# mLSTM and gated feed-forward on one core: the second group's queries are transposed by VectorE from squares, and its scores move behind block 9

## The chip, the cores and the metric

The kernel runs on one core of a Trainium2 chip. The core has a matrix engine (TensorE, "PE" in the profile, whose weight loads are listed as "PEld"), a vector engine (VectorE, "DVE"), a scalar engine (ScalarE, "ACT"), GpSimd ("POOL") and a queue engine, SyncE ("SP"), which here only issues DMA transfers. The metric is the device time of one execution, in microseconds (us). Before the change it is 505.11 us, the median of three runs (504.91 to 505.61).

## The reference

An mLSTM cell goes over 768 time steps for 4 x 8 heads of width 40. Its output, joined over the heads into 3072 tokens of width 320, goes through a gated feed-forward block of width 1536.

```python
for t in range(S):
    m_new = np.maximum(f_gate[:, :, t] + m, i_gate[:, :, t])
    f_stab = np.exp(f_gate[:, :, t] + m - m_new)
    i_stab = np.exp(i_gate[:, :, t] - m_new)
    m = m_new
    C = f_stab[:, :, None, None] * C + i_stab[:, :, None, None] * np.einsum('bhd,bhe->bhde', vt, kt)
    n = f_stab[:, :, None] * n + i_stab[:, :, None] * kt
    h_tilde = np.einsum('bhde,bhe->bhd', C, qt)
    nq = np.einsum('bhd,bhd->bh', n, qt)[:, :, None]
    y[:, :, t] = o * h_tilde / np.maximum(np.abs(nq), 1.0)      # o: sigmoid of o_gate
...
x = y.transpose(0, 2, 1, 3).reshape(B * S, H * D)
g = x @ w_gate
return (g * (1.0 / (1.0 + np.exp(-g))) * (x @ w_val)) @ w_out
```

The cell's inputs are 32-bit floats, the three feed-forward weights 64-bit floats.

## The kernel before

**Stages.** Time is cut into six groups of 128 steps, 0 to 5. A group's tokens (4 batches x 128 steps = 512) go through the cell and then through the feed-forward block. The kernel writes out the order of every engine's work by hand: the feed-forward products of one group are the frame, and the cell's steps for the next group are put between them. The change is in the first frame, group 0's hidden products, into which group 1's cell is put.

**The frame.** `hidden(0, m)` is block m of twelve: ten matrix products (five chunks of x, gate and value half each) of 64 x 128 weights by 512 tokens into two PSUM banks (tile `gv_ps`, line 808), then Silu on ACT (line 813, into `tmp`) and the product with the value half on DVE (line 814, into `h_sb`). There are four such banks, so block m needs the banks that line 814 of block m - 2 has read. `first` is a list of steps issued between a block's matrix products and its Silu; `slots[m]` are steps issued after block m. `project_all` then makes group 0's output product (line 825), with more of the cell of groups 1 and 2 between its twelve parts (`after`).

**Weights.** The 64-bit weights are loaded in eleven pieces (`piece_load`): the gate part on SP's queue, the value part on POOL's. A piece of the later gate and value weights holds two blocks; piece 7 holds blocks 10 and 11, pieces 8 to 10 the output weights. A block is then turned into 32-bit floats in three steps: `scale` (two ACT instructions, lines 249 and 251, which read the piece and so wait for its load), `join` (two on DVE, 258 and 259) and `rounded` (one, line 266, on POOL or on DVE). `convert` is all three. Two raw buffers are shared by the pieces: piece 9 can be loaded when piece 7 has been scaled, piece 10 when piece 8 has.

**Group 1's cell in the frame.** k and q are loaded in their natural layout (128 steps on the partitions, heads and features along the row; line 139, rows of 160 bytes, two DMAs each). `turn_one` transposes them on TensorE, 16 transposes for each half P of the heads (line 378, tile `tp_kq`), and ACT copies the four banks to `kT` and `qT` (line 156). The weights of the attention come in `w_sb`, which is loaded by broadcast from `M_dram` (line 552, issued by SP after a small table has landed there); DVE caps it (`weights_cap`, line 570), subtracts (`weights_sub`, 559) and ACT takes the exponential (577). `do_scores` is 64 small matrix products of kT and qT (line 411, into four banks `sp`), `do_weigh` multiplies them into `w_sb` on DVE (line 418). `weigh_values` (POOL, line 422) weights v; `do_add` makes the state's products (line 437), `do_state` adds them (DVE, 461), `do_decayed` decays the state (POOL, 454); `do_intra` (478) and `do_inter` (468) make the outputs, `do_gather` joins them.

**Squares.** For groups 2 to 5, q is loaded in another form: `load_squares` issues, for each of the two heads of a pair, four DMAs with rows of 128 bytes and four with rows of 32 bytes (line 395), so that every 32 x 32 piece lies where VectorE can transpose it in place of TensorE; `turn_squares` is two VectorE transposes of 128 x 1024 (line 401). `q_sq` is the same memory as `q_sb`.

**The queues.** SP issues its DMAs in order. There are eight completion semaphores, taken in turn, so a DMA's issue waits for the landing of the one eight places before it. The order around the change is: k (2 DMAs), w_sb (2), q (2), the gate part of piece 7, v (2), pieces 8 and 9, o (2), group 2's q squares (8), piece 10, squares (8), group 2's w_sb (2).

## Time and profile before

| what | value |
|---|---|
| median of 3 runs | 505.11 us (504.91 to 505.61) |
| the profiled execution | 504.85 us, of which 503.1 us are its span |
| TensorE busy | 498.6 us, 99% of the span |
| VectorE, GpSimd, ScalarE busy | 333.2, 261.1, 209.2 us |
| granted TensorE clock | 1.00 in every stretch asked for from 24 to 108 us |
| group 0's hidden products, line 808 | first at 25.8 us, last at 86.1 us; 53.8 us busy |
| q transposes of group 1 on TensorE | 65.57 to 66.92 us |
| VectorE transposes, line 401 | 16, about 1.22 us each, first at 108.6 us |

The profile is one execution taken by the hardware profiler. Each row of a timeline gives the start and the duration, the engine, the line of the kernel, the operation with its tiles (`out<-in`), the shape and the number of instructions merged into the row; in brackets stands how long the engine was idle before and what ended that wait. An instruction's 32-bit product counts twice ("x20" for ten). The weight loads (PEld) run ahead of their products, and a small gap of 0.23 us between them is their normal step. In the slices of the page each digit is a busy share in tenths of 12.6 us. "SPq" rows are DMAs being issued; their time includes waiting for room in the queue.

### The profile page before, as it was taken

How to read it: one execution, taken by the hardware profiler on the slowest of the kernel's cores; microseconds unless marked ns; L12 is line 12 of the kernel's file. 1: busy time of each engine (PE TensorE's matmuls, PEld its weight loads, DVE VectorE, ACT ScalarE, POOL GpSimd, SP SyncE). 2: the span in 40 equal slices, each digit the busy share in tenths (PEclk: the TensorE clock that was granted, in tenths of full speed). 3: DMA queues.
4: the chain of work that ended last, by engine and by line, in shares of the span. 5: the costliest groups of instructions: out<-in, count | busy, mean ns of one | idle time of the engine just before them, and what ended most of it. 6: DMA issues, size and time to landing. Idle time of an engine off the chain costs nothing.

```text
span 503.1 us, 14945 instructions
## 1 busy us (share of the span) xinstructions
PE 498.6 (99%) x6361; PEld 424.4 (84%) x6361; DVE 333.2 (66%) x542; ACT 209.2 (42%) x406; POOL 261.1 (52%) x292
## 2 busy tenths in 40 slices
PE   9999999999999999999999999999999999999997
PEld 4856555767889899888899888899888899988897
DVE  5889869889998587578376677467468464233421
ACT  4776784476262266323247312339311330223210
POOL 3753525458876925465723357643267650176710
PEclk9999999999999999999999999999999999999999
DMA  9999998797607982404991502991101100000001
GB/s 145 194 231 244 160 210 215 169 167 115 88 3 120 157 85 52 44 3 68 165 115 45 67 3 47 161 128 27 42 3 25 32 1 27 27 1 1 1 14 39
DMA packets 184938, 43.29 MB, mean 86 GB/s; under 512 B 173128, under 2 KB 180312, under 8 KB 184360
## 3 DMA queue, kind: packets, MB, share of 16 engines
q1 hardware_dynamic: 183396, 38.00, 48.0%
q0 software_dynamic: 1344, 4.28, 3.6%
q8 instruction: 50, 0.82, 0.7%
q14 instruction: 16, 0.13, 0.1%
q10 hardware_dynamic: 132, 0.07, 0.0%
HBM read 35.68 MB, written 4.01 MB: 79 GB/s over the span
## 4 chain that ended last, share of the span: by engine, by line
PE 97%; DVE 1%; ACT 1%; issue 0%; DVEq 0%
PE gv_x L978 26%; PE o_ps L879 22%; PE gv_y L978 21%; PE gv_ps L808 10%; PE o_ps L825 5%; PE inter L468 2%; PE sp L411 2%; PE intra L478 2%; PE o_ps L884 1%; PE add L437 1%; PE tp_kq L378 1%; PE sp L641 1%; PE tp_x L543 1%; PE wps L609 1%; PE burn L587 0%; PE wps L613 0%
## 5 line engine op out<-in xcount | busy, mean ns | idle before, releaser
L978 PE MATMUL gv_x<-xT,wgv_sb 64*128 64x256 f32 x720 | 89.1, 377 | 0.0
L978 PEld LDWEIGHTS gv_x<-xT,wgv_sb 64*128 64x128 f32 x720 | 69.3, 187 | 8.1 <-issue 0.2
L879 PE MATMUL o_ps<-wo_sb,h_sb 128*128 128x160 f32 x456 | 63.9, 300 | 0.0
L879 PEld LDWEIGHTS o_ps<-wo_sb,h_sb 128*128 128x128 f32 x456 | 62.3, 190 | 1.7 <-issue 1.7
L1026 ACT ACTIVATE h_sb<-gv_x 128x256 f32<-128x256 f32 x30 | 11.5, 384 | 116.3 <-PE gv_x L978 116.3
L808 PE MATMUL gv_ps<-xT,wgv_sb 64*128 64x512 f32 x240 | 53.8, 596 | 0.0
L808 PEld LDWEIGHTS gv_ps<-xT,wgv_sb 64*128 64x128 f32 x240 | 26.7, 187 | 22.6 <-issue 14.9
L978 PE MATMUL gv_y<-xT,wgv_sb 64*128 64x256 f32 x360 | 43.9, 376 | 0.0
L978 PE MATMUL gv_y<-q_sb,wgv_sb 64*128 64x256 f32 x360 | 43.9, 376 | 0.0
L422 POOL TENSOR_TENSOR vw_sb<-v_sb,w_sb 128x656 f32<-128x656 f32 x10 | 14.6, 1464 | 51.0 <-ACT w_sb L574 38.1
L978 PEld LDWEIGHTS gv_y<-xT,wgv_sb 64*128 64x128 f32 x360 | 34.9, 187 | 4.0
L978 PEld LDWEIGHTS gv_y<-q_sb,wgv_sb 64*128 64x128 f32 x360 | 34.9, 187 | 4.0
L574 ACT ACTIVATE w_sb<-w_sb,g_T 128x64 f32<-128x64 f32 x128 | 31.0, 334 | 0.0
L978 PE MATMUL gv_x<-q_sb,sw 64*128 64x256 f32 x240 | 30.9, 376 | 0.0
L879 PE MATMUL o_ps<-wT,S 128*128 128x160 f32 x216 | 30.2, 299 | 0.0
L879 PEld LDWEIGHTS o_ps<-wT,S 128*128 128x128 f32 x216 | 29.6, 190 | 0.0
L1019 POOL TENSOR_TENSOR tmp<-tmp 128x512 f32<-128x512 f32 x15 | 20.0, 1334 | 16.8 <-DVE tmp L1018 16.8
L999 POOL TENSOR_TENSOR h_sb<-x_sb 128x512 f32<-128x512 f32 x12 | 15.7, 1306 | 24.6 <-ACT x_sb L998 24.6
L999 POOL TENSOR_TENSOR h_sb<-tmp 128x512 f32<-128x512 f32 x13 | 16.5, 1269 | 21.5 <-ACT tmp L998 21.5
L846 POOL TENSOR_TENSOR S<-h_sb 128x256 f32<-128x256 f32 x30 | 22.6, 755 | 9.2 <-DVE h_sb L999 7.3
L1018 DVE TENSOR_TENSOR x_sb<-x_sb,gv_y 128x1024 f32<-128x1024 f32 x15 | 18.1, 1205 | 13.9 <-PE gv_y L978 11.6
L825 PE MATMUL o_ps<-wo_sb,h_sb 128*128 128x320 f32 x96 | 27.1, 438 | 0.0
(238 smaller groups left out, 1004.7 us busy)
## 6 DMA issues: line engine op xcount, KB each, us to landing
w_sb<-M_dram SPq DMA_DIRECT2D x8, 512.0 KB, 6.6
raw<-in_moe_w_out_dram SPq DMA_DIRECT2D x3, 1280.0 KB, 7.1
v_sb<-in_v_dram SPq DMA_DIRECT2D x11, 320.0 KB, 9.4
o_sb<-in_o_gate_dram SPq DMA_DIRECT2D x11, 320.0 KB, 5.0
k_sb<-in_k_dram SPq DMA_DIRECT2D x9, 320.0 KB, 7.3
x_sq<-k_sb SPq DMA_DIRECT2D x64, 40.0 KB, 2.8
q_sb<-in_q_dram SPq DMA_DIRECT2D x32, 64.0 KB, 3.7
out_dram<-tmp SPq DMA_DIRECT2D x24, 80.0 KB, 1.7
```

The lines of the kernel that those rows point to most:

```text
L411: nc.tensor.matmul(sp[two][keys(n, P, i), a, :], lhsT=kT[feats(two), P * UA + a, half(i)], rhs=qT[feats(two), P * UA + a, half(i)], start= ...
L422: eng.tensor_tensor(vw_sb[:, heads(P)], v_sb[:, heads(P)], w_sb[:, heads(P), last].to_broadcast([128, UH, D1]), op=ALU.mult)
L574: nc.scalar.activation(w_sb[:, h], w_sb[:, h], AF.Exp, bias=g_T[:, n, h:h + 1], scale=-1.0)
L808: nc.tensor.matmul(ps[i], lhsT=wgv_sb[half(i), m, kc, :], rhs=x[half(i), kc, :], start=(kc == 0), stop=(kc == NKC - 1))
L825: nc.tensor.matmul(ps[u], lhsT=hid(g, m)[:, ts(u, L)], rhs=wo_sb[:, m, :], start=(m == 0), stop=(m == NFC - 1))
L846: eng.tensor_tensor(S1[:, k], lo[:, second_half], hi[:, second_half], op=ALU.add)
L879: nc.tensor.matmul(node[x][:, i], lhsT=lhs(k)[:, ts(i, L)], rhs=rhs(k), start=start and k == 0 and i == 0, stop=stop and k == KH - 1, skip ...
L978: nc.tensor.matmul(ps[:, i, cols], lhsT=lhs(c)[half(i)], rhs=rhs(c)[half(i)], start=start and c == 0, stop=stop and c == n - 1, skip_group ...
L999: (nc.vector if k == KH - 1 else nc.gpsimd).tensor_tensor(h_sb[:, 2 * k + 1], uw[:, 0], uw[:, 1], op=ALU.mult)
L1018: nc.vector.tensor_tensor(uw, uw, y, op=ALU.add)
L1019: nc.gpsimd.tensor_tensor(uw[:, :, second_half], uw[:, :, second_half], uw[:, :, first_half], op=ALU.add)
L1026: nc.scalar.activation(h[:, first_half], x[:, 0, first_half], AF.Silu)
```

## The change

Group 1's q is loaded as squares: eight DMAs behind block 2's steps, behind the k loads and ahead of w_sb, and eight behind block 3's, in place of two; the transposes on TensorE in the middle of block 8 (with the parameter `amid` that put them there) and their four ACT copies are gone, and two VectorE transposes stand behind block 7, after `weights_exp`. POOL no longer clears `q_sb` behind block 8 (the rows beyond the 40 features are read by no product). `do_scores` and `do_weigh` for group 1 move from behind block 8 to behind block 9. The conversion of block 10, which was issued whole ahead of block 8's Silu, has only its `scale` and `join` there; its `rounded` comes behind block 8's product of line 814, still on DVE.

```diff
-    def hidden(g, m, first=(), amid=()):
+    def hidden(g, m, first=()):
...
-            if kc == 3:
-                for f in amid:
-                    f()
...
-    on_vector = (9, 10)
-    ahead = {0: [], 1: [3], 2: [4], 3: [5], 4: [6], 5: [7], 6: [8], 7: [9], 8: [10], 9: [], 10: [], 11: []}
+    on_vector = (9,)
+    ahead = {0: [], 1: [3], 2: [4], 3: [5], 4: [6], 5: [7], 6: [8], 7: [9], 8: [], 9: [], 10: [], 11: []}
...
-        2: [run(late_maxima), run(M_store, G), run(load_all, k_sb, k, 1)],
-        3: [run(late_decay), run(weights_load, 1), run(load_all, q_sb, q, 1)],
+        2: [run(late_maxima), run(M_store, G), run(load_all, k_sb, k, 1), run(load_squares, q_sq, q, 1, (0,))],
+        3: [run(late_decay), run(weights_load, 1), run(load_squares, q_sq, q, 1, (1,))],
...
-        7: [run(weights_sub, 1, 0), run(weights_sub, 1, 1), run(weights_exp, 0), run(weights_exp, 1), run(weigh_values, G, 0),
-            run(weigh_values, G, 1)],
-        8: [run(nc.gpsimd.memset, q_sb, 0.0), run(do_scores, 1), run(piece_load, 9), run(load_all, o_sb, o_gate, 1),
-            run(do_weigh, 0), run(do_weigh, 1)],
-        9: [run(join, 11), run(rounded, 11, V), run(do_decayed, 2)],
+        7: [run(weights_sub, 1, 0), run(weights_sub, 1, 1), run(weights_exp, 0), run(weights_exp, 1),
+            run(turn_squares, q_sq, qT), run(weigh_values, G, 0), run(weigh_values, G, 1)],
+        8: [run(rounded, 10, V), run(piece_load, 9), run(load_all, o_sb, o_gate, 1)],
+        9: [run(do_scores, 1), run(do_weigh, 0), run(do_weigh, 1), run(join, 11), run(rounded, 11, V), run(do_decayed, 2)],
...
-    amid = {8: [run(turn_one, P, q_sb, qT, (A, A)) for P in range(2)]}
...
-        first += {9: [run(scale, 11)], 10: [run(scale, 12), run(join, 12)], 11: [run(convert, 13)]}.get(m, [])
-        hidden(0, m, first, amid.get(m, ()))
+        first += {8: [run(scale, 10), run(join, 10)], 9: [run(scale, 11)], 10: [run(scale, 12), run(join, 12)], 11: [run(convert, 13)]}.get(m, [])
+        hidden(0, m, first)
```

## The prediction

> **What bounds the kernel now.** First the page: span, busy time, the slices, the chain that ended last.

> ```profile
> span 503.1 us, 14945 instructions
> ...
> PE 498.6 (99%) x6361; PEld 424.4 (84%) x6361; DVE 333.2 (66%) x542; ACT 209.2 (42%) x406; POOL 261.1 (52%) x292
> ...
> DMA  9999998797607982404991502991101100000001
> ...
> PE 97%; DVE 1%; ACT 1%; issue 0%; DVEq 0%
> ```

> TensorE holds 97% of the chain, so a microsecond taken from it is a microsecond of the whole, as long as nothing else is late there. But a slice is 12.6 us: in the first eight or nine the DMA engines are nearly full too. So I read the timeline around the change (slices 5 to 9).

> ```profile
> 65.57 0.15 PEld L378 LDWEIGHTS tp_kq<-x_sq,q_sb 64*128 64x128 f32 x2 [0.23 <-issue]
> ...
> 66.92 0.31 PEld L808 LDWEIGHTS gv_ps<-xT,wgv_sb 64*128 64x128 f32 x4
> ...
> 68.20 2.03 ACT L156 COPY qT<-tp_kq 128x512 f32<-128x512 f32 x4
> 68.85 0.19 PEld L411 LDWEIGHTS sp<-qT,kT 40*64 40x64 f32 x2 [0.76 <-ACT qT L156]
> ...
> 70.74 0.79 ACT L249 ACTIVATE top<-raw 128x640 f32<-128x640 f32 x1 [0.51 <-DMA raw<-in_moe_w_gate_dram]
> 71.36 0.30 PEld L808 LDWEIGHTS gv_ps<-xT,wgv_sb 64*128 64x128 f32 x4
> ...
> 71.56 0.49 DVE L258 TENSOR_SCALAR wgv_sb<-top 128x640 uint32<-128x640 uint32 x1 [4.35 <-ACT top L249]
> ...
> 72.23 1.28 ACT L813 ACT_TABLE_LOAD   x1
> ...
> 73.05 1.71 DVE L266 CUSTOM_DVE_ANT_0 wgv_sb<-wgv_sb,low 128x1280 uint16<-128x1280 uint16 x1
> ...
> 73.53 0.60 ACT L813 ACTIVATE tmp<-gv_ps 128x512 f32<-128x512 f32 x1
> ...
> 75.33 0.25 PEld L808 LDWEIGHTS gv_ps<-xT,wgv_sb 64*128 64x128 f32 x2 [0.23 <-issue]
> ```

> Block 8 is cut by the transposes at 65.57 and resumes at 66.92; scores start at 68.85, block 9 at 71.36, block 10 at 75.33. Block 10's weights wait for a DMA (70.74) and are finished by DVE at 73.05 + 1.71 = 74.76, only 0.57 us before TensorE needs them. Next, SP's queue and the later place where TensorE meets a DMA again:

> ```profile
> 51.04 1.13 SPq L552 DMA_DIRECT2D w_sb<-M_dram  x2
> 52.22 5.56 SPq L139 DMA_DIRECT2D q_sb<-in_q_dram  x2
> 57.96 1.98 SPq L222 DMA_DIRECT2D raw<-in_moe_w_gate_dram  x1
> 59.99 9.73 SPq L139 DMA_DIRECT2D v_sb<-in_v_dram  x2
> ```

> ```profile
> 105.10 1.23 DVE L570 TENSOR_TENSOR w_sb<-w_sb,cap 128x1024 f32<-128x1024 f32 x1 [1.85 <-DMA w_sb<-M_dram]
> ...
> 107.73 2.40 POOL L266 TENSOR_TENSOR wo_sb<-wo_sb,low 128x640 int32<-128x640 int32 x1 [2.86 <-DVE wo_sb L259]
> ...
> 110.18 8.37 PEld L825 LDWEIGHTS o_ps<-wo_sb,h_sb 128*128 128x128 f32 x32 [0.41 <-POOL wo_sb L266]
> ```

> DVE waits 1.85 us for group 2's w_sb, the output weights' conversion stands behind that wait, and TensorE waits for it at 110.18.

> **The change, part by part.**

> *TensorE loses 32 transposes.* Pairs of weight loads step by 0.43 us. Without the cut, block 8's last four pairs take 65.57 to 67.29, block 9's ten to 71.59. The switch to small matmuls costs 0.52 (the last pair before the state products starts at 79.20, they at 80.15). 64 scores take 2.01, as the 64 state products do (80.15 to 82.16) and the third group's scores (130.24 to 132.26); here they took 2.51, since they waited for the qT copies. So block 10 could start at 72.11 + 2.01 = 74.12. The first two pairs after a switch take 0.54, not 0.86 (71.36, 71.90), so it would end at 74.12 + 4.30 - 0.32 = 78.10, against 75.33 + 4.30 = 79.63: a gain of 1.53 us, the most this change has on TensorE.

> *DVE gains two transposes,* 2 x 1.22 (L401 qT, x8, mean 1222 ns) = 2.44 us, behind weights_sub, which ends at 67.20. DVE stood idle from there to 71.56 (the 4.35 above), so they cost nothing while q is there by then. Scores need qT at 72.11; 67.20 + 2.44 = 69.64. *ACT loses* the 2.03 us of qT copies, but it waited for the gate weights anyway (0.51): nothing. *POOL loses* a 1.80 us memset; nothing on the path waits for POOL there: nothing.

> *Block 10's rounding moves behind block 8's product.* ACT's scaling of block 10 starts at T, now 70.74. It holds ACT until the table load at T + 1.49; the Silu of block 8 ends at 74.13 = T + 3.39; the product L814 (0.69) then stands ahead of the rounding L266, which was done beside the Silu before. L266 takes 0.83 alone (63.27) and 1.71 beside POOL's value weighting (72.35 for 3.57). Ready: T + 4.08 + 0.83 to 1.71 = T + 4.9 to T + 5.8; POOL covers about its first half, I take T + 5.5. With T unchanged that is 76.2, where TensorE could start at 74.12: it waits 2.1 us, more than the 1.53 gained. This is the step that decides; to keep the whole gain, T must be 68.6 or earlier, and the exponentials that ACT does first end at 68.29.

> *SP: two q DMAs become sixteen.* Eight go ahead of w_sb, eight between w_sb and the gate weights. Each DMA waits for the landing of the one eight before it. The eighth waits for the second k load (issued 30.68, landed after 21.4, 52.1), w_sb #1 for the first square (about 53). So w_sb is issued at about 53.5 instead of 51.04 and lands some 2.5 us later, near 60.3; DVE's cap, now at 59.52, starts 0.8 late. Behind it stand block 9's rounding (now done at 64.10, needed at 67.29: 3.2 us of cover) and the exponentials, which then end at 69.1. The last two squares wait for w_sb's landing, so the gate load is issued at about 61 instead of 57.96. That is not yet a loss: from 61.6 to 64.5 the DMA engines carried the val weights alone (q0 at 95%) and the gate packets came after, 65 to 68. T moves by what the DMA engines have to do before. Old q: 3560 packets in 4.0 us (57.3 to 61.3, share 155%), so 4.6 us for 4096. New: 4096 of 128 bytes and 4096 of 32. The same loads of group 2: 2105 packets, nearly all of 128 bytes, in 1.8 us (93.8 to 95.6, share 95%); 2131 small ones in 2.6 us at 62% share, 1.6 us of engine time, and 1850 in 3.2 us at 32%, 1.0 us. So 3.0 us a half if SP runs ahead, 6.0 in all, 1.4 more than now, less the hole between k and w_sb (51 to 53, share 45%: 1.1 us), which the first half fills: +0.3. If the packets come no faster than in the sparse rows, 2 x (1.8 + 2.6) = 8.8 us: 4.2 - 1.1 = +3.1. If the gate packets run beside the val packets, T falls, but not below the exponentials' end: 69.1, -1.6. I take +0.5, near the engine-time row, since in this window there is a backlog ahead and SP can push early: T = 71.2.

> [...] If the count alone set the time, 8192 packets at the old 890 per us would be 9.2 us, and T would be 3.5 us later; the 128-byte row (1170 per us) does not yet show that.

> *Sum on TensorE.* Ready at 71.2 + 5.5 = 76.7, 2.6 us after 74.12; less 1.53 gained: +1.05 at the end of block 10. Behind it the state products, block 11's weights and so on follow TensorE or have a microsecond of room. At 110.18 TensorE waited 0.41 for POOL; its loads there step by 0.27 with 0.19 busy, so about 0.3 is a true stall, which takes up 0.3: +0.75. The same place works the other way: its chain starts from w_sb's landing (105.0), reached by SP through a full DMA queue. Had TensorE kept its 1.53, it would wait there, unless group 2's w_sb came earlier too. In the profiled execution 504.85 + 0.75 = 505.6; the median shown is 0.26 above it: **505.9**.

> **Rivals.**

> *The gain is kept (faster).* The gate packets share the DMA engines with the val packets instead of following them, and the whole queue up to group 2's w_sb moves up by as much. For: from 40 to 44 us, when both queues had weights, they moved 307 GB/s, against 186 from 61.6 to 64.5. Against: it is the sum of bytes that group 2's w_sb waits for, and that does not shrink. With T = 69.1 and 5.0 behind it, block 10 starts at 74.1 and keeps the 1.53; with group 2's w_sb 1.3 earlier, the end is 505.1 - 1.3 = 503.8. It becomes a gain of 0.2% when both come 1.0 us earlier.

> *The DMA queue becomes the bound (slower).* T moves by the +3.1 above. Then block 10 starts at 79.3: 5.2 - 1.53 - 0.3 = +3.4, 508.5. For: group 2's second eight took SP 8.78 us (88.95), and 5.88 the first; with 7 us for each half, w_sb and gate come late by that. Against: there they stood behind 1.3 MB of output weights. From T + 0.75 on this is slower by over 0.2%.

> *DVE is blocked by a late q.* If the sixteenth square lands after 71.5, DVE's transposes hold back block 10's conversion. That square is issued near 61 and such loads landed within 2.1 to 4.4 us (median); 4 us more behind the val packets still leave 2 us. In the same case as the last.

> **How the numbers follow.** 0.2% is 1.0 us, about what a measurement of this kernel can tell from no change. Given back, 0.55: centre +0.75, with -0.2 to +2 from rounding alone or contended and T at +0.3 to +1.5; 0.32 of it within 1.0 us, 0.23 above. Kept, 0.17: 0.13 below -1.0, 0.04 within. Queue bound or q late, 0.28, all above. Together 0.13, 0.36, 0.51. The likeliest gives 505.9; its own range is 504.9 to 507.1. The range 504.0 to 508.2 leaves out half of the kept case and some of the bound one.

> **What would show it.** The scores' wait on ACT is gone and they take 2.0 us; DVE L401 appears twice ahead of block 10's L258. Right: a stall of 2 to 3 us on the matmuls' loads after the scores, ended by DVE's rounding, and the scaling of block 10 (ACT L249) waiting for the gate weights at 70.5 to 72. Wrong, to the fast side: no stall there, L249 before 69.5, and group 2's cap on DVE a microsecond earlier than 105.1. Wrong, to the slow side: w_sb landing after 62, or DVE waiting for q_sb ahead of L401.

## The result, and the profile after it

The changed kernel takes 509.76 us (median of six runs, 508.13 to 510.84) against 505.49 us for the kernel before beside it: ratio 1.0079, 95% interval 1.0054 to 1.0104. It is slower by 4.3 us. (The ratios here and below are worked out over the runs of both kernels and differ a little from the quotient of the two medians.) I had forecast 505.9 (504.0 to 508.2), so the sign was right and the size was not; the range did not hold it. The profiled execution took 508.92 us. Lines of the changed kernel are three lower than before (808 is 805, 813 is 810, 814 is 811, 825 is 822).

The page first: span, busy time, granted clock by slice, and the chain that ended last.

```profile
span 507.2 us, 14895 instructions
...
PE 499.1 (98%) x6329; PEld 425.2 (84%) x6329; DVE 334.4 (66%) x544; ACT 207.1 (41%) x402; POOL 258.7 (51%) x291
...
PEclk9999998999999999999999999999999999999999
...
PE 95%; DMA 2%; DVE 1%; ACT 1%; issue 0%; ACTq 0%; DVEq 0%
```

TensorE has 32 transposes less and is still busy 0.5 us longer, a DMA now holds 2% of the chain, and one slice has a granted clock below full speed (the 8 in the seventh, 76 to 89 us). The slice is right behind the changed place. The timeline there:

```profile
61.45 2.36 DVE L570 TENSOR_TENSOR w_sb<-w_sb,cap 128x1024 f32<-128x1024 f32 x2 [1.59 <-DMA w_sb<-M_dram]
...
68.82 2.36 DVE L401 STREAM_TRANSPOSE qT<-q_sb 128x1024 f32<-128x1024 f32 x2
...
72.05 0.78 ACT L249 ACTIVATE top<-raw 128x640 f32<-128x640 f32 x1 [2.05 <-DMA raw<-in_moe_w_gate_dram]
72.36 1.96 PEld L411 LDWEIGHTS sp<-qT,kT 40*64 40x64 f32 x128 [0.76 <-issue]
...
75.48 0.69 DVE L811 TENSOR_TENSOR h_sb<-tmp,gv_ps 128x512 f32<-128x512 f32 x1 [1.27 <-ACT tmp L810]
76.08 1.58 DVE L266 CUSTOM_DVE_ANT_0 wgv_sb<-wgv_sb,low 128x1280 uint16<-128x1280 uint16 x1
...
77.78 0.33 PEld L805 LDWEIGHTS gv_ps<-xT,wgv_sb 64*128 64x128 f32 x4 [3.46 <-ACT tmp L810]
77.81 6.26 PE L805 MATMUL gv_ps<-xT,wgv_sb 64*128 64x512 f32 x20 [3.35 <-DVE wgv_sb L266]
...
79.96 0.40 PEld L805 LDWEIGHTS gv_ps<-xT,wgv_sb 64*128 64x128 f32 x2 [0.45 <-issue]
80.81 0.40 PEld L805 LDWEIGHTS gv_ps<-xT,wgv_sb 64*128 64x128 f32 x2 [0.45 <-issue]
...
84.00 1.96 PEld L437 LDWEIGHTS add<-vw_sb,k_sb 64*64 64x64 f32 x128 [0.76 <-DVE wo_sb L258]
```

The scores run without a wait, from 72.36 to 74.32. Then TensorE stands for 3.4 us, until VectorE's rounding (L266) of block 10 ends at 77.66, and that chain starts at 72.05 with a wait for the gate weights. This is the stall that I had forecast, longer. The second thing I had not forecast: the pairs of weight loads of block 10 step by 0.85 us (79.96, 80.81) instead of 0.43, and the block needs 6.2 us from its start to the state products at 84.00 (4.8 before, from 75.33 to 80.15). The kernel before, at the end of block 10:

```profile
78.77 0.19 PEld L808 LDWEIGHTS gv_ps<-xT,wgv_sb 64*128 64x128 f32 x2 [0.24 <-issue]
79.20 0.19 PEld L808 LDWEIGHTS gv_ps<-xT,wgv_sb 64*128 64x128 f32 x2 [0.24 <-issue]
80.15 1.96 PEld L437 LDWEIGHTS add<-vw_sb,k_sb 64*64 64x64 f32 x128 [0.76 <-DVE wgv_sb L259]
```

```profile
71.55:74.96 3.41, 2.91 (x134) 2.01 (x130) 1.32 (x2) 2.88 (x4) 1.11 (x1) 1.00 1.44 174
74.96:78.37 3.41, 0.56 (x4) 0.39 (x6) 2.89 (x4) 2.31 (x4) 3.11 (x4) 1.00 1.07 365
78.37:81.78 3.41, 3.41 (x12) 1.60 (x10) 3.38 (x6) 0.00 (x0) 0.58 (x1) 0.50 0.94 337
81.78:85.20 3.42, 3.42 (x95) 2.04 (x92) 2.77 (x5) 2.64 (x4) 0.00 (x0) 1.00 1.12 220
```

In the stretch that holds the stall TensorE is busy for 0.56 us of 3.41; through the whole next one it gets half its clock. Half of 3.41 us is 1.7 us of work not done.

SP's queue, and the place at 105 to 110 us where TensorE met a DMA before:

```profile
54.19 1.13 SPq L552 DMA_DIRECT2D w_sb<-M_dram  x2
55.36 8.35 SPq L395 DMA_DIRECT2D q_sb<-in_q_dram  x8
63.88 2.25 SPq L222 DMA_DIRECT2D raw<-in_moe_w_gate_dram  x1
66.18 4.96 SPq L139 DMA_DIRECT2D v_sb<-in_v_dram  x2
```

```profile
107.01 1.21 DVE L570 TENSOR_TENSOR w_sb<-w_sb,cap 128x1024 f32<-128x1024 f32 x1
...
109.55 12.41 PEld L822 LDWEIGHTS o_ps<-wo_sb,h_sb 128*128 128x128 f32 x47
```

The second eight squares hold SP for 8.35 us; the gate load is issued at 63.9 (57.96 before). At 109.55 TensorE no longer waits for POOL, and the cap waits for no load: TensorE is late enough itself.

The 4.1 us of the span, by stages: block 0 starts 0.3 us later (26.2, 25.9 before), a place ahead of everything that the change touches; from there to the state products of group 1 it takes 3.55 us more (84.00 - 80.15 - 0.3); 0.2 of it is gone by the state products of group 2 (122.67 against 118.99); the rest of the span is 0.4 us longer. And the 3.55 add up: -1.53 (the gain as forecast) + 3.4 (stall) + 1.7 (half clock) = 3.57.

### The profile page after: what moved, and what is told of

It reads as the page before. It is cut to its first block, busy times and chain, and to the rows that moved or that the text cites. A ratio compares the mean times of both kernels' runs of the same rounds, so it can differ in the third digit from the quotient of the medians.

```text
span 507.2 us, 14895 instructions
## 1 busy us (share of the span) xinstructions
PE 499.1 (98%) x6329; PEld 425.2 (84%) x6329; DVE 334.4 (66%) x544; ACT 207.1 (41%) x402; POOL 258.7 (51%) x291
## 4 chain that ended last, share of the span: by engine, by line
PE 95%; DMA 2%; DVE 1%; ACT 1%; issue 0%; ACTq 0%; DVEq 0%
PE gv_x L975 26%; PE o_ps L876 21%; PE gv_y L975 21%; PE gv_ps L805 9%; PE o_ps L822 5%; PE inter L468 2%; PE intra L478 2%; PE sp L411 2%; DMA raw<-in_moe_w_gate_dram 2%; PE o_ps L881 1%; PE add L437 1%; DMA x_sq<-in_i_gate_dram 1%; PE tp_kq L378 1%; PE sp L641 1%; PE tp_x L543 1%; PE wps L613 1%
## 5 line engine op out<-in xcount | busy, mean ns | idle before, releaser
L876 PE MATMUL o_ps<-wo_sb,h_sb 128*128 128x160 f32 x456 | 63.9, 300 | 0.0
L805 PE MATMUL gv_ps<-xT,wgv_sb 64*128 64x512 f32 x240 | 55.2, 610 | 3.4 <-DVE wgv_sb L266 3.4
L805 PEld LDWEIGHTS gv_ps<-xT,wgv_sb 64*128 64x128 f32 x240 | 28.7, 192 | 26.3 <-issue 14.2
L1015 DVE TENSOR_TENSOR tmp<-tmp,gv_y 128x1024 f32<-128x1024 f32 x15 | 18.1, 1205 | 13.7 <-PE gv_y L975 12.0
```

Of the source, the lines that this page charges most:

```text
L805: nc.tensor.matmul(ps[i], lhsT=wgv_sb[half(i), m, kc, :], rhs=x[half(i), kc, :], start=(kc == 0), stop=(kc == NKC - 1))
L876: nc.tensor.matmul(node[x][:, i], lhsT=lhs(k)[:, ts(i, L)], rhs=rhs(k), start=start and k == 0 and i == 0, stop=stop and k == KH - 1, skip ...
L1015: nc.vector.tensor_tensor(uw, uw, y, op=ALU.add)
```

## The experiments

The two theories at the start. Theory A: the mechanism of the prediction, a late block 10, and on top of it a clock that halves because TensorE stands still. Rival B: the clock is a thing of its own (chip, other work), and the stall alone or the squares' load alone explain the time. Ratios are against the kernel before on the same chip. The medians of the kernel before lie between 505.5 and 507.0 in the four sets of runs, so stages and clocks say more than times across them.

**The rounding first again.** Block 10's whole conversion stands ahead of block 8's Silu, as before the change; all else is as changed.

```diff
-    on_vector = (9,)
-    ahead = {0: [], 1: [3], 2: [4], 3: [5], 4: [6], 5: [7], 6: [8], 7: [9], 8: [], 9: [], 10: [], 11: []}
+    on_vector = (9, 10)
+    ahead = {0: [], 1: [3], 2: [4], 3: [5], 4: [6], 5: [7], 6: [8], 7: [9], 8: [10], 9: [], 10: [], 11: []}
...
-        8: [run(rounded, 10, V), run(piece_load, 9), run(load_all, o_sb, o_gate, 1)],
+        8: [run(piece_load, 9), run(load_all, o_sb, o_gate, 1)],
...
-        first += {8: [run(scale, 10), run(join, 10)], 9: [run(scale, 11)], 10: [run(scale, 12), run(join, 12)], 11: [run(convert, 13)]}.get(m, [])
+        first += {9: [run(scale, 11)], 10: [run(scale, 12), run(join, 12)], 11: [run(convert, 13)]}.get(m, [])
```

> The changed kernel, with one part undone: block 10 is converted whole ahead of block 8's Silu again, so that its rounding on DVE does not stand behind block 8's product. Theory (the order on ACT and DVE makes the stall, and a stall of about 3.4 us makes the granted TensorE clock drop, which costs as much again): the gate weights still land near 72, the rounding is done by about 75.9, block 8's product follows and frees the banks at 76.6; TensorE stalls 2.3 us behind the scores instead of 3.4 and the clock stays at 1.00. About 506.5 against 505.5 of the kernel before. Rival (the squares in SP's queue cost the time, wherever the rounding stands): 509 to 510, as the changed kernel. Rival (the clock drops after any stall): about 508.5, clock 0.995.

Measured: 508.82, ratio 1.0039 (1.0022 to 1.0055). The gate weights landed later in this run (scaling at 73.20).

```profile
77.35 1.35 PEld L805 LDWEIGHTS gv_ps<-xT,wgv_sb 64*128 64x128 f32 x5 [2.34 <-ACT top L249]
...
83.77 1.96 PEld L437 LDWEIGHTS add<-vw_sb,k_sb 64*64 64x64 f32 x128 [0.76 <-DVE wgv_sb L266]
```

The stall shrinks to 2.3 us, as expected; the half clock stays, against the theory and as the second rival has it (77.32 to 80.73 at 0.50, with TensorE busy 1.24 us of the 3.41 before it; ten of twelve runs at 0.993 to 0.997). So moving the rounding back wins about half of the loss: the order on VectorE is a cause of the stall, but the lateness of the weights alone is enough for stall and clock.

**Silu first.** The other order: block 8's Silu and product first, the whole conversion behind them.

```diff
-        8: [run(rounded, 10, V), run(piece_load, 9), run(load_all, o_sb, o_gate, 1)],
+        8: [run(convert, 10, V), run(piece_load, 9), run(load_all, o_sb, o_gate, 1)],
...
-        first += {8: [run(scale, 10), run(join, 10)], 9: [run(scale, 11)], 10: [run(scale, 12), run(join, 12)], 11: [run(convert, 13)]}.get(m, [])
+        first += {9: [run(scale, 11)], 10: [run(scale, 12), run(join, 12)], 11: [run(convert, 13)]}.get(m, [])
```

> The changed kernel, but block 10 is converted whole behind block 8's Silu and product: ACT loads its table and makes the Silu while it waits for the gate weights, instead of after them. Theory (the serial chain of scaling, table load, Silu, product, rounding behind the gate weights' landing makes the stall): with the gate weights at 72, the rounding is done at about 75.3, TensorE stalls 0.9 us instead of 3.4, the clock stays at 1.00; 4 us or more faster than the changed kernel: 505 (503.9 if group 2's w_sb does not bind, up to 506 if it does). Rival (the landing of the gate weights sets the time): 508 or more.

Measured: 508.57, ratio 1.0028 (1.0008 to 1.0048). The expected short stall did not come about: the gate weights landed at 72.8 (71.9 in the changed kernel), the scaling started at 72.96, the rounding took 1.71 beside POOL, and TensorE waited 2.44 us for it (block 10's loads at 77.06). What this variant adds is a spread within one kernel: of its twelve runs five had a clock of 0.999 or 1.00 (median 506.68) and six one of 0.997 (median 508.6). The medians of the same program with and without one interval of half clock differ by 1.9 us; that is a weak measure, since two of the five at full clock took 508.80 and 510.09.

**Scores made twice.** The 64 scores are made a second time into the same banks, to give TensorE work where it stood.

```diff
...
-        9: [run(do_scores, 1), run(do_weigh, 0), run(do_weigh, 1), run(join, 11), run(rounded, 11, V), run(do_decayed, 2)],
+        9: [run(do_scores, 1), run(scores_again, 1), run(do_weigh, 0), run(do_weigh, 1), run(join, 11), run(rounded, 11, V), run(do_decayed, 2)],
```

> The changed kernel, and its 64 scores of group 1 are made a second time, into the same banks, with the same values: 2.0 us more work for TensorE, put into the stall ahead of block 10. Theory (the stall itself costs some 2 us and the clock's drop behind it 2 us and more): block 10 starts at the same time, near 77.8, its weight-load pairs step by 0.43 us and not by 0.85, the granted clock is 1.00, and the time falls by about 2 us to 507.5, with more work. Rival (block 10 is slow for another reason: its loads or the stall's end): block 10 takes 6.2 us as in the changed kernel, 509.5. Rival (TensorE is simply busy with one thing more): 2.0 us slower, 511.7.

Measured: 512.02, ratio 1.008 (1.005 to 1.011). It does not test the theory, since the stall was not filled:

```profile
72.67 2.99 PEld L411 LDWEIGHTS sp<-qT,kT 40*64 40x64 f32 x194 [0.76 <-issue]
...
78.33 1.02 PEld L411 LDWEIGHTS sp<-qT,kT 40*64 40x64 f32 x62 [2.67 <-issue]
```

TensorE stopped for 2.67 us in the middle of the repeated scores, which wait for nothing there. From 74 to 80 us the transfers include one packet of instructions (16 KB, at 75.6, 1.36 us), one of 51 such packets in the run. Whether the stop has to do with it was not tried.

**The stall filled.** After that, a fill of few and long instructions: 14 dummy products of zeros ahead of the scores, into a bank that the scores overwrite.

```diff
...
-    def do_scores(n):
+    def do_scores(n, filled=0):
         for P in range(2):
-            live["sp", P] = scores(n, P)
+            sp = duo("sp")
+            for x in range(filled):
+                nc.tensor.matmul(sp[x % 2], lhsT=junk[:, 0:128], rhs=junk, start=True, stop=True)
+            filled = 0
+            live["sp", P] = scores(n, P, [x.rearrange("p (a t) -> p a t", t=SUB) for x in sp])
...
-        9: [run(do_scores, 1), run(do_weigh, 0), run(do_weigh, 1), run(join, 11), run(rounded, 11, V), run(do_decayed, 2)],
+        9: [run(do_scores, 1, 14), run(do_weigh, 0), run(do_weigh, 1), run(join, 11), run(rounded, 11, V), run(do_decayed, 2)],
```

> After the change, with 14 dummy products (128x128 weights, 512 columns, all zeros, about 0.21 us each, 3.0 us in all) put on TensorE between block 9 and the scores; they write into a bank that the scores then overwrite. Block 10's weights come as late as in after, so the time up to block 10 does not change; but TensorE has work where it stood still. Theory (the halved clock behind block 10's start is a consequence of TensorE standing still): no stretch at a granted clock below 1, block 10 takes 4.3 us instead of 6.2, state products near 82.1 instead of 84.0; time 2 us under after, 507.5 (1.004 of before). Rival (the clock drop comes from something else in the change, such as when work is late, not from idle TensorE): clock 0.995 to 0.997 as before, 509.5.

Measured: 509.36, ratio 1.0045 (1.0028 to 1.0062); ten of twelve runs at a clock of 1.00. The timeline, and two of the grid's stretches:

```profile
74.15 2.71 PEld L1038 LDWEIGHTS <-junk 128*128 128x128 bf16 x14 [0.76 <-issue]
...
77.28 1.96 PEld L411 LDWEIGHTS sp<-qT,kT 40*64 40x64 f32 x128 [0.42 <-DVE h_sb L811]
...
79.31 4.56 PE L805 MATMUL gv_ps<-xT,wgv_sb 64*128 64x512 f32 x20
...
83.80 1.96 PEld L437 LDWEIGHTS add<-vw_sb,k_sb 64*64 64x64 f32 x128 [0.76 <-DVE wgv_sb L266]
```

```profile
73.73:77.14 3.41, 3.36 (x17) 1.29 (x14) 2.13 (x4) 3.38 (x5) 2.15 (x2) 1.00 1.25 252
77.14:80.55 3.41, 3.41 (x135) 2.65 (x136) 3.41 (x5) 0.87 (x2) 2.58 (x3) 1.00 0.99 312
```

Block 10 starts as late as ever (79.31, in a run whose scores were due 1.8 us later than in the changed kernel, for a reason far ahead of the change, a half-clock interval from 25.94), but takes 4.5 us instead of 6.2. The dummies took 3.19 us (from 74.16, thirteen of the 14 in the trace); I had put them at 3.0. All twelve runs of the changed kernel (these six and six more below) have a clock of 0.993 to 0.997. Useless work made this kernel faster: the ratio falls from 1.0079 to 1.0045. The intervals of these two, from two chips, just touch; that of the changed kernel again (1.0068 to 1.0109) lies clear. That is theory A, and B falls.

**A stall in the kernel before.** Nothing of the change; only dummy instructions on VectorE (an OR with zero) ahead of the rounding of block 10, six in one kernel (shown), three in the other.

```diff
             lo, dst = blocks.pop(j)
+            for _ in range(6 if j == 10 else 0):
+                nc.vector.tensor_scalar(dst, dst, scalar1=0, scalar2=None, op0=ALU.bitwise_or)
```

> The kernel before, with six dummy VectorE instructions of 0.48 us (an OR with zero, in place) ahead of the rounding of block 10: nothing of the change is in it, only its stall. Rounding starts near 76.2 instead of 73.05, block 8's product ends near 77.7, so TensorE waits 2.4 us ahead of block 10. Theory (a stall of this length halves the granted clock for 3.4 us, which costs 1.7 us more): about +4 us on the span up to 80, 0.3 taken up at 110: ratio 1.007, clock 0.997. Rival (the clock drop belongs to the change): +2.1, ratio 1.004, clock 1.00.

> As the last, with three dummy instructions: TensorE waits about 1.0 to 1.2 us ahead of block 10. Theory (a short stall leaves the clock alone; two of three stalls of 2.3 us or more were followed by the half clock): +0.9 us, ratio 1.002, clock 1.00. Rival (any stall beyond the usual switch of 0.5 us halves it): +2.6, ratio 1.005, clock 0.997.

Measured: with six 513.68, ratio 1.0122 (1.0097 to 1.0147), clock 0.990 to 0.997 in all runs; with three 513.67, ratio 1.0117 (1.0083 to 1.0152). The size was missed, and neither theory nor rival gave these times: I had priced the dummies at 0.48 us by the shift of the same shape (L258), and on 32-bit signed integers they took 1.27 (7.66 for six) to 1.69 us (5.08 for three). So TensorE stands for 5.2 and 3.0 us, and a short stall was not measured. (The two in three of the second expectation was a wrong count: in the five profiles until then, the half clock followed each stall of 2.3 us or more.) What the first does tell: the kernel before, with a stall of 5.2 us, got the half clock too (two stretches in its profile, 80.1 to 87.0). And the profiled run with three is an exception that helps. It has a stall of 3.0 us, a clock of 1.00 throughout and 509.62 us, while the other five runs have 0.993 to 0.997 and 513.1 to 515.1. Its grid cuts the stall in two:

```profile
74.81:78.22 3.41, 1.96 (x10) 0.58 (x6) 3.38 (x2) 1.61 (x3) 3.41 (x3) 1.00 0.92 302
78.22:81.63 3.41, 1.87 (x8) 1.25 (x10) 3.27 (x6) 0.00 (x0) 1.99 (x2) 1.00 1.04 368
81.63:85.05 3.42, 3.42 (x35) 1.88 (x33) 3.35 (x6) 0.50 (x1) 0.00 (x0) 1.00 0.92 162
```

**The changed kernel again,** unchanged, on another chip, the one of the scores' move alone and of the two variants with POOL's queue.

> The changed kernel once more, on the chip of the next runs, so that they can be compared with it. Theory (stall of 3 us or more ahead of block 10, then one or two intervals of 3.4 us at half clock): ratio 1.006 to 1.010, clock 0.993 to 0.997 in nearly every run. Rival (the clock drop was a matter of the first chip): ratio 1.003, clock 1.00.

Measured: 510.89, ratio 1.0088 (1.0068 to 1.0109), all six runs at 0.993: two intervals each, as here, where the stall lies across two stretches and each is followed by half clock.

```profile
73.33:76.75 3.42, 1.84 (x128) 1.70 (x118) 1.66 (x3) 3.39 (x5) 1.62 (x2) 1.00 1.31 230
76.75:80.16 3.41, 1.39 (x4) 0.90 (x6) 3.41 (x5) 1.45 (x3) 3.16 (x3) 0.50 0.97 310
80.16:83.57 3.41, 3.41 (x10) 1.48 (x8) 3.34 (x6) 0.61 (x1) 0.00 (x0) 0.50 1.07 372
```

Stretches of the grid at full clock with little TensorE work, and the clock of the one that follows (the first microseconds of a run, for which no clock is recorded, are left out):

| kernel | stretch from | TensorE busy, us of 3.41 | clock of the next stretch |
|---|---|---|---|
| half of the squares on POOL, cap behind (below) | 72.37 | 0.00 | half |
| changed | 74.96 | 0.56 | half |
| half of the squares on POOL (below) | 71.70 | 1.08 | half |
| Silu first | 74.61 | 1.11 | half |
| rounding first | 73.91 | 1.24 | half |
| before, six dummies | 76.73 | 1.26 | half |
| without the small rows (below) | 109.20 | 1.37 | half |
| scores twice | 76.42 | 1.51 | half |
| without the small rows, end of the program | 501.73 | 1.69 | full |
| stall filled (early, no part of the change) | 22.53 | 1.74 | half |
| changed, again | 73.33 | 1.84 | half |
| before, three dummies | 78.22, 74.81 | 1.87, 1.96 | full |
| changed, again (early) | 22.13 | 2.08 | full |
| without the small rows, cap behind (below) | 73.00 | 2.45 | full |

**The scores' move alone.** The kernel before, with only the scores and their weighting behind block 9.

```diff
-        8: [run(nc.gpsimd.memset, q_sb, 0.0), run(do_scores, 1), run(piece_load, 9), run(load_all, o_sb, o_gate, 1),
-            run(do_weigh, 0), run(do_weigh, 1)],
-        9: [run(join, 11), run(rounded, 11, V), run(do_decayed, 2)],
+        8: [run(nc.gpsimd.memset, q_sb, 0.0), run(piece_load, 9), run(load_all, o_sb, o_gate, 1)],
+        9: [run(do_scores, 1), run(do_weigh, 0), run(do_weigh, 1), run(join, 11), run(rounded, 11, V), run(do_decayed, 2)],
```

> The kernel before with one part of the change alone: the scores and their weighting behind block 9 instead of 8 (q still loaded in two DMAs, turned on TensorE in the middle of block 8; block 10 converted as before). The scores no longer wait 0.57 us for the copies of qT. Theory (block 10 is held by block 8's product on VectorE, which ends at 75.35 and is ruled by the gate weights' landing): block 10 starts where it did, at 75.3; ratio 1.000, clock 1.00. Rival (the move itself starts a stall like that of after): ratio 1.004, clock 0.997.

Measured: 506.28, ratio 1.0005 (0.9991 to 1.0019). As expected: it costs and gains nothing.

```profile
70.46 0.81 ACT L249 ACTIVATE top<-raw 128x640 f32<-128x640 f32 x1
...
73.51 1.96 PEld L411 LDWEIGHTS sp<-qT,kT 40*64 40x64 f32 x128 [0.76 <-issue]
...
74.42 0.68 DVE L814 TENSOR_TENSOR h_sb<-tmp,gv_ps 128x512 f32<-128x512 f32 x1
...
75.53 4.56 PE L808 MATMUL gv_ps<-xT,wgv_sb 64*128 64x512 f32 x20
```

The rounding and block 8's product are done by 75.1, the scores by 75.5: the two chains meet within half a microsecond. TensorE and the gate weights' chain are nearly balanced here, so a gain on TensorE alone has about 0.4 us to go.

**Without the small rows.** The changed kernel without the eight q loads of 32-byte rows for group 1. (Features 32 to 39 of q are then left out of this group's scores.)

```diff
-            for s in range(2):
+            for s in range(1 if c == 1 else 2):
```

> The changed kernel without the eight q DMAs of 32-byte rows for group 1 (features 32 to 39 of q are not loaded for that group, so this part of its scores is left out). Theory (the squares hold up SP's queue and so the gate weights): the gate load is issued near 58 instead of 63.9, its weights land about 1.5 us earlier, at 70.5, the stall falls to about 2 us and the clock stays at 1.00: 506. Rival (the stall comes from the order of the conversion alone): the weights land at 72 as before, 509 to 510.

Measured: 508.26, ratio 1.0008 (0.9984 to 1.0033).

```profile
69.44 0.80 ACT L249 ACTIVATE top<-raw 128x640 f32<-128x640 f32 x1 [0.34 <-DMA raw<-in_moe_w_val_dram]
...
72.90 1.96 PEld L411 LDWEIGHTS sp<-qT,kT 40*64 40x64 f32 x128 [0.76 <-issue]
...
74.92 4.56 PE L805 MATMUL gv_ps<-xT,wgv_sb 64*128 64x512 f32 x20
...
79.42 1.96 PEld L437 LDWEIGHTS add<-vw_sb,k_sb 64*64 64x64 f32 x128 [0.76 <-DVE wgv_sb L259]
...
111.67 1.21 PEld L822 LDWEIGHTS o_ps<-wo_sb,h_sb 128*128 128x128 f32 x5 [2.55 <-POOL wo_sb L266]
```

With them gone the gate part is issued at 56.7 and lands at 65.9 (63.9 and 71.9 in the changed kernel), and the value part lands last, at 69.2. There is no stall at block 10, no half clock there, and the state products come at 79.42, 53.0 us behind the start of block 0 (26.4); before the change it was 54.3. So the eight loads of small rows are what made the weights late (whether by their 4096 packets or by being eight transfers more, this run can't tell), and without them 1.3 of the 1.53 us are gained. But the time is no better: at 111.67 TensorE waits 2.6 us for the output weights' conversion, behind VectorE's wait of 4.1 us for group 2's `w_sb`, and the clock halves behind that stall.

**The cap behind the conversion.** That variant, with group 2's first cap behind the conversion of block 16 on VectorE. (The same features are left out.)

```diff
-        3: [run(do_divide, 1, 1), run(weights_cap, 0)],
+        3: [run(do_divide, 1, 1)],
-        4: [run(seam, 1, 0, (A, A, A, A)), run(convert, 16), run(weights_cap, 1), run(turn_squares, q_sq, qT)],
+        4: [run(seam, 1, 0, (A, A, A, A)), run(convert, 16), run(weights_cap, 0), run(weights_cap, 1), run(turn_squares, q_sq, qT)],
```

> The variant without group 1's eight small-row q loads (group 1's q features 32 to 39 are left out of its scores), and group 2's first cap of w_sb (VectorE, which waits for the load of w_sb) put behind the conversion of the output weights' block 16 instead of ahead of it. Theory (TensorE's gain of 0.7 us at block 10 was lost at 109 to 112 because that conversion stood behind the wait for w_sb): no stall of 2.6 us at 109, clock 1.00, time 0.7 to 1.0 us under before, ratio 0.998. Rival (other work of the cell for group 2 is late as well, and the wait only moves on): a stall of 2 us or more between 109 and 120, ratio 1.001 or above.

Measured: 507.65, ratio 1.001 (0.9985 to 1.0035), clock 1.00 or 0.999 in ten of twelve runs. The stall of 2.6 us at 109 to 112 is gone, with its half clock, and a shorter one stands at the next block, since that block's conversion now has both caps ahead of it:

```profile
116.11 4.07 PEld L822 LDWEIGHTS o_ps<-wo_sb,h_sb 128*128 128x128 f32 x16 [1.21 <-POOL wo_sb L266]
```

In this run the value part landed later too (scaling at 71.33) and block 10 waited 1.1 us. No gain can be measured. That is nearer to the rival, by which the wait moves on, though the stall is 1.2 us and not the 2 that it named.

**Half of the squares on POOL's queue.** The rounding first, and the second eight squares issued by POOL behind the value part, so that SP issues the gate part at once.

```diff
...
-        3: [run(late_decay), run(weights_load, 1), run(load_squares, q_sq, q, 1, (1,))],
+        3: [run(late_decay), run(weights_load, 1)],
...
-        6: [run(piece_load, 7, parts=VALUE)] + [run(turn_one, P, k_sb, kT, (A, A)) for P in range(2)] + [run(weights_cap, 0), run(weights_cap, 1), run(piece_load, 8)],
+        6: [run(piece_load, 7, parts=VALUE), run(load_squares, q_sq, q, 1, (1,), nc.gpsimd)] + [run(turn_one, P, k_sb, kT, (A, A)) for P in range(2)] + [run(weights_cap, 0), run(weights_cap, 1), run(piece_load, 8)],
```

> After, with the rounding of block 10 ahead of block 8's product again, and the second eight of group 1's squares issued by POOL behind the value part of piece 7 instead of by SP ahead of the gate part. SP issues the gate load near 55.5 instead of 63.9. Theory (the sixteen squares in SP's queue are what makes the gate weights late): the scaling of block 10 starts as soon as ACT has done the exponentials, near 70.3 instead of 72.05; block 8's product ends near 75, the stall ahead of block 10 is under 1 us and the clock stays at 1.00; state products near 79.5; the place at 109 takes the gain back: ratio 0.998 to 1.001. Rival (the squares are late instead, VectorE's transposes wait for q and hold the conversion): the stall stays at 2 us or more, clock 0.997, ratio 1.003 to 1.005.

Measured: 511.68, ratio 1.0108 (1.0085 to 1.013).

```profile
60.68 3.90 POOL L395 DMA_DIRECT2D q_sb<-in_q_dram  x6
70.17 1.29 POOL L395 DMA_DIRECT2D q_sb<-in_q_dram  x2 [5.60 <-DMA raw<-in_moe_w_val_dram]
70.60 0.79 ACT L249 ACTIVATE top<-raw 128x640 f32<-128x640 f32 x1 [0.55 <-DMA raw<-in_moe_w_val_dram]
...
75.55 2.37 DVE L401 STREAM_TRANSPOSE qT<-q_sb 128x1024 f32<-128x1024 f32 x2 [6.60 <-DMA q_sb<-in_q_dram]
...
76.91 3.53 PEld L411 LDWEIGHTS sp<-qT,kT 40*64 40x64 f32 x128 [4.96 <-issue]
```

The scaling starts at 70.60, as forecast for it, but the squares land at 75.4 (hence the wait of the transposes at 75.55), and now TensorE waits 5 us for q. The rival has the mechanism, at a higher price than it named. Two things hold q back. POOL issues six of its eight squares at once and the last two only at 70.17, after 5.6 us of waiting for the value part to land; that fits an issue that waits for the landing of the transfer eight places ahead, since the two value loads and six squares make eight. (In the trace of before, POOL's issues at 30.30 and 33.35 waited 0.74 and 1.84 us for a load of the value weights, which was the one eight places ahead.) And the DMA engines have little spare time around here (a share of 0.94 and more in the changed kernel's stretches from 71 to 85), so what is moved ahead can make another load late: in this run the gate part lands 7.3 us earlier than in the changed kernel (64.6), the value part 3.6 us later (70.4). An order in which POOL does not meet that wait was not tried.

**Both of these.** The last, with the cap behind the conversion.

> The last, and group 2's first cap of w_sb on VectorE behind the conversion of the output weights' block 16 instead of ahead of it, so that the conversion does not wait for that load. Theory (TensorE's gain is then kept): 0.5 to 1.0 us under the last, ratio 0.997 to 0.999. Rival (as in the variant without small rows, where this order gave nothing that could be measured): the same as the last within 0.5 us.

Measured: 513.94, ratio 1.0152 (1.0126 to 1.0177). The squares are late in the same way (transposes at 75.67, after 6.34 us of waiting), and with a stall of 5.5 us ahead of the scores this says nothing about the cap. Neither expectation came about.

None of the variants beats the kernel before.

## Why the prediction failed, point by point

- *TensorE loses 32 transposes: a gain of 1.53 us.* Right. The scores took 1.96 without a wait and ended at 74.32, which is 74.02 without the 0.3 us of the later start; I had 74.12. Without the small rows 1.3 us reached the state products.
- *VectorE, ACT and POOL: nothing.* Right. The transposes ran at 68.82 to 71.18, in VectorE's gap.
- *Block 10's rounding behind block 8's product: ready at T + 5.5.* Right: 77.66 with T = 72.05 is T + 5.6, with a rounding of 1.58 where T + 5.5 leaves it 1.42. With the old order the loss was half.
- *SP's queue: T = 71.2.* Mis-sized. T was 72.05, which without the later start is +1.0 instead of +0.5, inside the bounds given (-1.6 to +3.1). The working behind it was off by more: w_sb was issued at 54.2 instead of 53.5, the gate part at 63.9 instead of 61, and group 1's cap came 1.9 us later instead of 0.8. The row-based estimate of 3.0 us for a half missed what the loads of 32-byte rows cost in this queue: without their 4096 packets (0.13 MB) the gate part lands 6.0 us earlier. Against the kernel before, though, it lands only 1.3 us later (71.9 against 70.7), while it is issued 5.9 us later. The T + 3.5 that I had worked out from the packet count did not come about; why the landing moved so much less than the issue stays open.
- *The sum on TensorE: stall less gain, +1.05.* This is the step that failed. It counted the stall as waiting time alone. In the changed kernel the stall of 3.4 us was followed by 3.413 us at half clock, in other runs of it by two such intervals: 1.7 us each by the profile. The six runs of the changed kernel show it: three at a clock of 0.997 (one interval) average 508.72, three at 0.993 (two) 510.63, so one interval is worth 1.9 us. Without any it would be some 506.8 (508.72 less 1.9, an estimate), which the range held. With the stall filled, the ratio fell to 1.0045. The trace of before could not show this, as its clock is 1.00 throughout, and I did not weigh it.
- *0.3 us absorbed at 110.* About right: 0.2 us, and the stall at 110.18 is gone. The other half of that step, that TensorE could not keep its gain there, is shown by the variants without the small rows: 2.6 us of waiting at that place, and after the reordering 1.2 us at the next block.
- *The rivals.* "Kept" needed T near 69; the variant without the small rows had it (69.44, in a run whose block 0 started 0.6 later), kept 1.3 us at block 10 and lost it at 111. "The DMA queue is the bound" and "q late" were the right fear, and the variant with POOL's queue shows the second (q late by 5 us, in part by POOL's own wait); in the changed kernel itself it was the gate part that was late.

## What to carry to other kernels

A stall of TensorE in an otherwise dense stretch had a second price in this kernel: behind a stretch of the grid in which TensorE was busy for 1.84 us or less of 3.41, the next stretch ran at half clock in ten of eleven cases, 1.7 us more for each. So look for that behind a forecast stall of the lengths seen here (2.3 us and more) before calling a trade even; and where the stall could not be avoided, dummy products in it were cheaper than none (ratio 1.0045 against 1.0079). Where an engine and a chain of loads are balanced to half a microsecond, as here, work taken from the engine bought nothing that could be measured (1.0005 with the scores' move alone), and the loads that put sixteen transfers, eight of them of small rows, in the place of two were paid for by the gate part behind them in the queue (issued 5.9 us later than before, landed 1.3 us later).

## What the runs showed of the hardware that was not expected

- The half clock came in whole stretches of the grid: in the table above, 1.84 us or less of TensorE work in a stretch of 3.41 us was followed by half clock in ten of eleven cases; behind 1.87 us or more, at full clock, there was none. The same kernel ran with and without it (509.62 against 513.1 to 515.1 for the kernel before with three dummies). Busy time is not the whole measure. The eleventh case, 1.69 us of products with 128x128 weights at the end of the program, was followed by a stretch at full clock. And in the two runs with half of the squares on POOL, a stretch that was busy throughout, first with small scores and then with block 10, both at half clock (78.53 to 81.94, and 79.19 to 82.61), was followed by half clock again. What exactly is counted stays open.
- The kernel before had a clock below full in some runs too: on one chip two of its 29 runs had a mean of 0.997 (the mean of the profiled run of the changed kernel, with one interval of half clock), on another two of 17, and on a third four of 23 had 0.990 to 0.997.
- A VectorE operation with one scalar on 128 x 640 took 0.48 us on unsigned integers (a shift, L258, the mean of the eleven on `wgv_sb` in the trace of before; one of the six on `wo_sb` took 1.40) and 1.27 to 1.69 us on signed ones (an OR, in place). Which of the differences does it was not tried.
- TensorE stopped for 2.67 us in a row of products that waited for nothing, beside a packet of instructions of 1.36 us, in one profile. The cause was not tried.
